# Strassen stage of a two-layer expert network: ScalarE copies the sixth product's bank ahead of the first tile's relu

## The chip, the cores and the metric

The kernel runs on one core of one Trainium2 chip. The metric is the time of one execution of the whole program in microseconds; lower is better. The engines are named as in the profile: PE is TensorE (PEld its weight loads), DVE is VectorE, ACT is ScalarE, POOL is GpSimd, SP is SyncE.

## The reference

Three networks follow one another: pooled attention, a leaky two-layer network, and four experts whose outputs are added with weights. The change lies in the last one.

```
def _moe2_ref(x, domain_probs, w1, w2):
    p = domain_probs / (domain_probs.sum(-1, keepdims=True) + 1e-09)
    out = np.zeros((N, D))                  # N 1152, D 512, 4 experts, F 1024
    for e in range(E):
        h = np.maximum(x @ w1[e], 0.0)
        out += p[:, e:e + 1] * (h @ w2[e])
    return out
```

## The kernel before

Every matrix product is made in three parts: an operand is split into a high half, which ACT writes (helper `hi`, line 91), and the rest, which DVE or POOL subtracts (helper `lo`, line 98); then high times high, high times low and low times high are added up in PSUM. The instructions stand in each engine's queue in the order in which the program calls them; no scheduler moves them.

The expert stage takes the hidden columns in 16 pairs of tiles of 128 (`NPAIR`), numbered p, four pairs to an expert. For one pair the product x @ w1 is made by Strassen's scheme in the Winograd form: seven products of half size instead of eight. `product(p, name)` issues one: 12 weight loads and 12 matmuls of 288 columns (line 688), and the instructions that empty its bank pair. They run in the order P1, P5, P2, P6, P3, P7, P4, so P7 is the sixth and P4 the seventh.

PSUM has four bank pairs here: `x0` and `x1` (by p % 2), `v` and `z`. P1, P6, P7 and P4 of one pair add up in one x pair of banks; after each, its sum so far is copied out before the next is added:

- P1: ACT copies it to the first half of `ca` (line 694). P5: ACT copies it to `c5` (tile cc, line 696). P2: DVE adds its bank to the first half of `ca` (line 698).
- P6: ACT copies the x banks to the second half of `ca` (line 700). P3: DVE adds its bank to that half (line 702). Now `ca` holds the pair's first tile, f1: ACT writes its relu to the tile gg (line 704), and DVE the low part of it (line 705).
- P7: ACT copies the x banks to `cb` (line 707), and DVE adds `c5` (line 708).
- P4 adds into the same x banks, so its first matmul waits for the copy of line 707. Its bank and `cb` make the second tile, f2: ACT relu (line 712), DVE low part (line 713), once for each half.

The order of the products is a list written by the program. P4 of a pair does not follow its P7 at once. After a pair with odd p, P1 of the next pair stands between. After a pair with even p above 0, one of nine output tiles stands between (`second_moe2`, lines 728 to 730: 12 matmuls of 512 columns, with DVE adding the result to `oacc` on line 735), and the eight others follow P4. Pair 0 is like an odd one. In the last pair, p = 15, P4 comes straight after P7, and after it the last nine output tiles, which read both tiles of pairs 14 and 15.

Weights of later pairs are prepared between: `prep_w1` after P5 and P6 (ACT `hi` and DVE `lo`, tile ws), `sums_w1` on POOL (lines 651 to 654), `prep_w2` after P2 of the next pair, or after P7 in the last pair (ACT `hi`, POOL `lo`, tile bb).

Of the kernel before, what the change touches and what calls it, by code (L numbers as in the profile page):

```python
# [33 lines left out]
def f32(ap):  # L34
    return ap.bitcast(F32)
# [3 lines left out]
def tile_kernel(ctx: ExitStack, tc: tile.TileContext, q, k, v, w_in, w_out, probs, w1, w2, out):  # L39
    nc = tc.nc  # L40
    PE, ACT, DVE, POOL, SP = nc.tensor, nc.scalar, nc.vector, nc.gpsimd, nc.sync

    def at(name, off, shape, dt=F32R):

        return nc.alloc_sbuf_tensor_at(name, [128, *shape], dt, offset=BASE + 4 * off).ap()
# [40 lines left out]
    cb, c5 = at("cb", 50560, [SQ], F32), at("cc", 52384, [SQ], F32)  # L86
# [106 lines left out]
    with ExitStack() as actx:  # L193
# [247 lines left out]
        with tc.manual_schedule():  # L441
# [65 lines left out]
            for i, (n, t) in enumerate(tiles):  # L507
# [16 lines left out]
                if t in (1, 4, 6, 8):  # L524
                    name, w = {1: ("A1", 256), 4: ("A2", 320), 6: ("B1", 320), 8: ("B2", 256)}[t]
# [26 lines left out]
    def view(t, n=NC):  # L552
        return t.rearrange("p (c w) -> p c w", c=n)
# [124 lines left out]
    def product(p, name):  # L678
        x = f"x{p % 2}"
        tag, first = {"P1": (x, 1), "P6": (x, 0), "P7": (x, 0), "P4": (x, 0), "P5": ("v", 1), "P3": ("v", 0), "P2": ("z", 1)}[name]  # L680
        ps = banks[tag]
        part, i, operand = OPERAND[name]
        w, y = w1_t[p, part], yb[operand]
        for k in range(2):
            ks = slice(k * 128, (k + 1) * 128)
            for m, (wi, yi) in enumerate(((0, 0), (0, 1), (1, 0))):
                for c in range(2):
                    PE.matmul(ps[:, c, :HW], w[wi][:, i, ks], y[:, yi, k, c * HW:(c + 1) * HW],  # L688
                              start=bool(first and k == 0 and m == 0), stop=k == 1 and m == 2, skip_group_check=True)
        s = ps[:, :, :HW]  # L690
        f1, f2 = n1 + 2 * p, n1 + 2 * p + 1
        c1, c2 = view(ca[:, :SQ], 2), view(ca[:, SQ:], 2)
        if name == "P1":
            ACT.copy(c1, s)  # L694
        elif name == "P5":
            ACT.copy(view(c5, 2), s)
        elif name == "P2":
            DVE.tensor_tensor(c1, s, c1, op=ALU.add)
        elif name == "P6":
            ACT.copy(c2, s)  # L700
        elif name == "P3":
            DVE.tensor_tensor(c2, s, c2, op=ALU.add)
            gh, gl = g_t[f1] = tuple(gg_b[2 * p % 6][:, i] for i in range(2))
            ACT.activation(gh, ca, AF.Relu)
            DVE.scalar_tensor_tensor(gl, ca, 0.0, f32(gh), op0=ALU.max, op1=ALU.subtract)
        elif name == "P7":
            ACT.copy(view(cb, 2), s)  # L707
            DVE.tensor_tensor(cb, cb, c5, op=ALU.add)
        else:
            gh, gl = g_t[f2] = tuple(gg_b[(2 * p + 1) % 6][:, i] for i in range(2))  # L710
            for src, h, l in ((s, view(gh[:, :SQ], 2), view(gl[:, :SQ], 2)), (cb, gh[:, SQ:], gl[:, SQ:])):
                ACT.activation(h, src, AF.Relu)
                DVE.scalar_tensor_tensor(l, src, 0.0, f32(h), op0=ALU.max, op1=ALU.subtract)
# [70 lines left out]
    with tc.manual_schedule():  # L784

        order, pending = [], None
        for p in range(NPAIR):
            todo = [(product, p, x) for x in ("P1", "P5", "P2", "P6", "P3", "P7")]
            order.append(todo.pop(0))
            if pending:  # L790
                order.append(pending)
            order += todo
            pending = (product, p, "P4")
            if p % 2 == 0 and p:
                tiles2 = [(second_moe2, p // 2 - 1, t) for t in range(NTT)]
                order += [tiles2[0], pending, *tiles2[1:]]
                pending = None
# [11 lines left out]
        for what, *args in order:  # L809
            what(*args)  # L810
            if what is product:
                p, name = args
# [39 lines left out]
```

## Time and profile before

| what | value |
|---|---|
| runs, us | 866.94, 868.99, 868.78; median 868.78 |
| profiled execution, us | 866.99 |
| its span, first to last instruction, us | 865.2 |
| busy over the span | PE 829.0 us (96%), PEld 777.9 (90%), DVE 587.4 (68%), ACT 435.6 (50%), POOL 403.6 (47%) |
| mean granted TensorE clock | 0.988 of full |
| Strassen and output stage | from about 470 us to the end |

Busy time is a mean over three unlike stages, and a matmul's end is modelled, so PE's 96% does not say that PE never waits. How long PE really stood still is read from the weight loads: each matmul has one, they are issued at a steady pace, and a gap in that pace is time lost.

### The profile page before, as it was taken

The page shows a single profiled execution, that of the slowest core. Times are in us where ns is not written, and L with a number is a line of the kernel's source. Part 1 is how long each engine was busy: PE and PEld are TensorE (multiplying, and loading weights), DVE is VectorE, ACT ScalarE, POOL GpSimd, SP SyncE. Part 2 cuts the span into 40 slices and gives each one's busy share as a digit, 9 for nine tenths or more (in the row PEclk, how much of TensorE's full clock was granted, in tenths as well). Part 3 has the DMA queues.
Part 4 walks back from the last instruction along what each step waited for, and adds up shares of the span by engine and source line. Part 5 has one row for each costly group of instructions (what it writes and reads, how often), then busy time and mean ns, then how long its engine had stood idle before and what let it go on. Part 6 is the DMA issues. An engine that isn't in the chain of part 4 may idle for free.

```text
span 865.2 us, 13539 instructions
## 1 busy us (share of the span) xinstructions
PE 829.0 (96%) x5071; PEld 777.9 (90%) x5071; DVE 587.4 (68%) x964; ACT 435.6 (50%) x762; POOL 403.6 (47%) x362
## 2 busy tenths in 40 slices
PE   6899999999989799999999899999999999999998
PEld 5789999999989799999999888889898898889886
DVE  5989999999998989877866662625444352625342
ACT  4889999999875565443333541505142241506030
POOL 1678988898744678556551330505032331404020
PEclk7999999999999999999999999999999999999999
DMA  6446545654501223322120210202011110201012
GB/s 192 111 123 179 136 113 151 178 125 123 153 26 50 98 98 98 98 98 74 57 91 1 72 51 1 98 1 73 26 49 49 49 50 1 98 0 49 1 37 98
DMA packets 25153, 68.65 MB, mean 79 GB/s; under 512 B 2944, under 2 KB 7040, under 8 KB 25088
## 3 DMA queue, kind: packets, MB, share of 16 engines
q1 hardware_dynamic: 25088, 67.79, 26.3%
q8 instruction: 40, 0.66, 0.3%
q14 instruction: 25, 0.20, 0.1%
HBM read 48.91 MB, written 2.36 MB: 59 GB/s over the span
## 4 chain that ended last, share of the span: by engine, by line
PE 75%; DVE 15%; ACT 4%; issue 3%; DMA 1%; POOL 1%; SPq 0%; DVEq 0%; ACTq 0%; POOLq 0%
PE ps L688 16%; PE ps L728 8%; PE ps L729 8%; PE ps L730 8%; PE ps L346 7%; PE ps L413 6%; PE ps L386 5%; DVE e L349 4%; PE ps L585 3%; PE ps L586 3%; PE ps L587 3%; PE ps L187 3%; PE ps L188 3%; PE ps L189 3%; DVE tl L98 2%
## 5 line engine op out<-in xcount | busy, mean ns | idle before, releaser
L98 POOL TENSOR_TENSOR bb<-w2r,bb 128x512 fp32r<-128x512 f32 x32 | 44.9, 1424 | 284.1 <-ACT bb L91 284.1
L688 PE MATMUL ps<-yT,ws 128*128 128x288 f32 x768 | 114.4, 300 | 10.6 <-ACT cb L707 10.6
L688 PEld LDWEIGHTS ps<-yT,ws 128*128 128x128 f32 x768 | 106.4, 191 | 15.1 <-ACT cb L707 14.9
L735 DVE SCALAR_TENSOR_TENSOR oacc<-ps,pw,oacc 128x512 f32<-128x512 f32 x63 | 47.2, 750 | 102.6 <-PE ps L730 102.6
L365 POOL TENSOR_SCALAR e<-e,st 128x1152 f32<-128x1152 f32 x70 | 86.8, 1243 | 57.4 <-DVE st L363 49.8
L98 DVE TENSOR_TENSOR tl<-ps,th 128x384 fp32r<-128x384 f32 (+1 forms) x240 | 112.0, 503 | 1.7 <-ACT th L390 1.7
L728 PE MATMUL ps<-bb,gg 128*128 128x512 f32 x288 | 112.2, 390 | 0.0
L729 PE MATMUL ps<-bb,gg 128*128 128x512 f32 x288 | 112.2, 389 | 0.0
L730 PE MATMUL ps<-bb,gg 128*128 128x512 f32 x288 | 112.1, 389 | 0.0
L346 PE MATMUL ps<-k,qst 128*128 128x384 f32 x438 | 97.2, 354 | 11.9 <-DVE e L349 6.7
L349 DVE TENSOR_SCALAR_CACHE_REDUCE e<-ps 128x1152 f32<-128x1152 f32 x72 | 97.4, 1353 | 16.3 <-PE ps L346 14.5
L390 ACT CAST th<-ps 128x384 fp32r<-128x384 f32 (+1 forms) x240 | 91.1, 458 | 23.8 <-PE ps L386 22.2
L355 ACT ACTIVATE e<-e,st 128x1152 f32<-128x1152 f32 x72 | 91.1, 1265 | 4.4 <-DVE e L349 2.7
L346 PEld LDWEIGHTS ps<-k,qst 128*128 128x128 f32 x438 | 77.4, 195 | 17.2 <-DVE e L349 11.9
L694 ACT COPY ca<-ps 128x576 f32<-128x576 f32 x16 | 10.3, 641 | 163.4 <-PE ps L688 155.0
L386 PE MATMUL ps<-ident,e 128*128 128x128 f32 x648 | 84.4, 275 | 3.8 <-POOL e L365 2.0
L688 PE MATMUL ps<-yB,ws 128*128 128x288 f32 x576 | 84.4, 296 | 0.0
L386 PEld LDWEIGHTS ps<-ident,e 128*128 128x128 f32 x648 | 75.0, 141 | 9.7 <-POOL e L365 5.0
L688 PEld LDWEIGHTS ps<-yB,ws 128*128 128x128 f32 x576 | 79.8, 189 | 0.5
L98 DVE TENSOR_TENSOR ws<-wf,ws 128x768 fp32r<-128x768 f32 (+1 forms) x32 | 41.5, 1297 | 55.5 <-ACT ws L91 55.5
L187 PE MATMUL ps<-xh,a 128*128 128x384 f32 x192 | 65.1, 339 | 4.1 <-DVE gf L564 4.1
L585 PE MATMUL ps<-g,b 128*128 128x384 f32 x192 | 64.4, 335 | 0.7 <-DVE gf L564 0.3
(126 smaller groups left out, 1728.2 us busy)
## 6 DMA issues: line engine op xcount, KB each, us to landing
wa<-in_w_in SPq DMA_DIRECT2D x16, 512.0 KB, 3.5
wb<-in_w_out SPq DMA_DIRECT2D x16, 512.0 KB, 4.3
wf<-in_w SPq DMA_DIRECT2D x32, 256.0 KB, 3.5
w2r<-in_w SPq DMA_DIRECT2D x16, 512.0 KB, 3.5
qst<-rq SPq DMA_DIRECT2D x28, 288.0 KB, 4.5
rv<-in_v SPq DMA_DIRECT2D x8, 576.0 KB, 5.3
rk<-in_k SPq DMA_DIRECT2D x7, 576.0 KB, 6.1
rq<-in_q SPq DMA_DIRECT2D x7, 576.0 KB, 4.7
```

The costliest lines, as they stand in the source:

```text
L98: eng.tensor_tensor(dst, src, f32(high), op=ALU.subtract)
L187: PE.matmul(ps[:, c, :CW], wh[:, k_], src_h[:, k_, cs], start=k_ == 0, stop=False)
L346: PE.matmul(ps[:, c, :CW], x, y, start=m == 0, stop=m == len(mms) - 1)
L349: DVE.tensor_scalar(e, ps[:, :, :CW], -0.5 / float(D) ** 0.5, None, op0=ALU.mult, op1=ALU.min, accum_out=st[:, 0:1])
L355: ACT.activation(e, e, AF.Exp, bias=st[:, 0:1], scale=-1.0, accum_out=st[:, 1:2])
L386: PE.transpose(ps[:, j], e[:, (3 * g + j) * 128:(3 * g + j + 1) * 128], ident)
L390: ACT.copy(h, ps[:, :, s0:s0 + w])
L585: PE.matmul(ps[:, c, :CW], wh, gh[:, cs], start=f == fs[0], stop=False)
L688: PE.matmul(ps[:, c, :HW], w[wi][:, i, ks], y[:, yi, k, c * HW:(c + 1) * HW], start=bool(first and k == 0 and m == 0), stop=k == 1 and m = ...
L728: PE.matmul(ps, gh[:, ts_], wh, start=f == fs[0], stop=False)
L729: PE.matmul(ps, gh[:, ts_], wl, start=False, stop=False)
L730: PE.matmul(ps, gl[:, ts_], wh, start=False, stop=f == fs[-1])
```

## The change

In `product`, the relu of the first tile and its low part (lines 704 and 705) move from the branch of P3 to the branch of P7, behind the copy of P7's bank. The same instructions are issued, as many as before.

```diff
         elif name == "P3":
             DVE.tensor_tensor(c2, s, c2, op=ALU.add)
+        elif name == "P7":
+
+            ACT.copy(view(cb, 2), s)
             gh, gl = g_t[f1] = tuple(gg_b[2 * p % 6][:, i] for i in range(2))
             ACT.activation(gh, ca, AF.Relu)
             DVE.scalar_tensor_tensor(gl, ca, 0.0, f32(gh), op0=ALU.max, op1=ALU.subtract)
-        elif name == "P7":
-            ACT.copy(view(cb, 2), s)
             DVE.tensor_tensor(cb, cb, c5, op=ALU.add)
```

The lines below move down by one: the copy is now line 705, the relu 707, the low part 708, the add of c5 709.

ACT's queue from P6 of pair 1 to P4 of pair 1, where P1 of pair 2 stands between P7 and P4 (L694 is that P1's copy; ws are weights, gg the relu's tiles):

```order
 L700 COPY ca<-ps 128x576
 L91 CAST ws_131<-wf_144 128x1024
-L704 ACTIVATE gg_138<-ca 128x1152
-L707 COPY cb<-ps 128x576
-L694 COPY ca<-ps 128x576
-L712 ACTIVATE gg_139<-ps 128x576
-L712 ACTIVATE gg_139<-cb 128x576
+L705 COPY cb<-ps 128x576
+L707 ACTIVATE gg_138<-ca 128x1152
+L694 COPY ca<-ps 128x576
+L713 ACTIVATE gg_139<-ps 128x576
+L713 ACTIVATE gg_139<-cb 128x576
```

The copy and the relu have changed places; the copy of the next pair's P1 and the two relus of the second tile stay behind both. It is the same in each of the 16 pairs.

ACT's queue at the end of the last pair, before (bb are the output weights of pair 15):

```order
552 L700 COPY ca<-ps 128x576
553 L704 ACTIVATE gg_136<-ca 128x1152
554 L707 COPY cb<-ps 128x576
555 L91 CAST bb_134<-w2r 128x512
556 L91 CAST bb_135<-w2r 128x512
557 L712 ACTIVATE gg_137<-ps 128x576
558 L712 ACTIVATE gg_137<-cb 128x576
```

and with the change:

```order
552 L700 COPY ca<-ps 128x576
553 L705 COPY cb<-ps 128x576
554 L707 ACTIVATE gg_136<-ca 128x1152
555 L91 CAST bb_134<-w2r 128x512
556 L91 CAST bb_135<-w2r 128x512
557 L713 ACTIVATE gg_137<-ps 128x576
558 L713 ACTIVATE gg_137<-cb 128x576
```

Here the two casts of the output weights stand behind the relu, which now stands behind the copy. The order on DVE, PE, POOL and SP is as before.

## Rows read from the trace of the kernel before

**Rows 1.** Page, chain that ended last: share of the span by engine.

```profile
PE 75%; DVE 15%; ACT 4%; issue 3%; DMA 1%; POOL 1%; SPq 0%; DVEq 0%; ACTq 0%; POOLq 0%
```

**Rows 2.** Waits, 465 to 866 us: engine, tile, line <- releaser: us, times, longest.

```profile
PEld ps L688 <- ACT cb L707: 14.9, 15, 2.1
...
PE ps L688 <- ACT cb L707: 10.6, 9, 1.9
```

**Rows 3.** Timeline, PE's weight loads: start us, us, instruction [idle before <- releaser].

```profile
590.16 1.66 PEld L688 LDWEIGHTS ps<-yT,ws 128*128 128x128 f32 x12
591.76 1.66 PEld L688 LDWEIGHTS ps<-yB,ws 128*128 128x128 f32 x12
594.74 3.21 PEld L688 LDWEIGHTS ps<-yT,ws 128*128 128x128 f32 x24 [1.32 <-ACT cb L707]
597.89 1.66 PEld L688 LDWEIGHTS ps<-yB,ws 128*128 128x128 f32 x12
```

**Rows 4.** Timeline of ACT in the same place.

```profile
592.99 1.16 ACT L704 ACTIVATE gg<-ca 128x1152 fp32r<-128x1152 f32 x1 [2.52 <-DVE ca L702]
594.06 0.62 ACT L707 COPY cb<-ps 128x576 f32<-128x576 f32 x1
595.75 0.64 ACT L694 COPY ca<-ps 128x576 f32<-128x576 f32 x1 [1.07 <-DVE gg L705]
596.63 0.65 ACT L712 ACTIVATE gg<-ps 128x576 fp32r<-128x576 f32 x1 [0.23 <-PE ps L688]
...
598.23 0.64 ACT L696 COPY cc<-ps 128x576 f32<-128x576 f32 x1 [0.38 <-PE ps L688]
...
599.50 1.15 ACT L91 CAST bb<-w2r 128x512 fp32r<-128x512 f32 x2
601.43 0.64 ACT L700 COPY ca<-ps 128x576 f32<-128x576 f32 x1 [0.79 <-PE ps L688]
```

**Rows 5.** Weight loads of P4 behind an output tile.

```profile
607.29 1.63 PEld L688 LDWEIGHTS ps<-yT,ws 128*128 128x128 f32 x12 [0.38 <-ACT cb L707]
```

**Rows 6.** Weight loads of the first pair's P4, with P1 of the next pair ahead.

```profile
479.97 1.66 PEld L688 LDWEIGHTS ps<-yB,ws 128*128 128x128 f32 x12
483.76 4.74 PEld L688 LDWEIGHTS ps<-yT,ws 128*128 128x128 f32 x24 [2.13 <-ACT cb L707]
```

**Rows 7.** Windows: us, PE, PEld, DVE, ACT, POOL busy (count), PE clock, DMA.

```profile
484.00:486.00 2.00, 2.00 (x10) 2.00 (x10) 1.24 (x2) 0.64 (x1) 0.00 (x0) 0.50 0.00 0
```

**Rows 8.** Timeline of ACT at the end of the last pair.

```profile
833.42 1.17 ACT L704 ACTIVATE gg<-ca 128x1152 fp32r<-128x1152 f32 x1 [1.82 <-DVE ca L702]
834.49 0.62 ACT L707 COPY cb<-ps 128x576 f32<-128x576 f32 x1
835.07 1.14 ACT L91 CAST bb<-w2r 128x512 fp32r<-128x512 f32 x2
```

**Rows 9.** Weight loads there: P7, P4, and an output tile's eleventh.

```profile
832.23 1.66 PEld L688 LDWEIGHTS ps<-yT,ws 128*128 128x128 f32 x12
835.16 1.61 PEld L688 LDWEIGHTS ps<-yT,ws 128*128 128x128 f32 x12 [1.27 <-ACT cb L707]
...
838.95 0.19 PEld L729 LDWEIGHTS ps<-bb,gg 128*128 128x128 f32 x1
```

**Rows 10.** Timeline of POOL there: low parts of the output weights.

```profile
828.99 2.53 POOL L98 TENSOR_TENSOR bb<-w2r,bb 128x512 fp32r<-128x512 f32 x2 [32.15 <-ACT bb L91]
835.77 3.13 POOL L98 TENSOR_TENSOR bb<-w2r,bb 128x512 fp32r<-128x512 f32 x2 [4.24 <-ACT bb L91]
```

**Rows 11.** Timeline of DVE there.

```profile
834.62 1.36 DVE L705 SCALAR_TENSOR_TENSOR gg<-ca,gg 128x1152 fp32r<-128x1152 f32 x1 [1.23 <-ACT gg L704]
835.89 1.85 DVE L708 TENSOR_TENSOR cb<-cb,cc 128x576 f32<-128x576 f32 x1
```

**Rows 12.** Timeline of POOL in the middle: two adds of one size.

```profile
591.23 1.60 POOL L652 TENSOR_TENSOR wf<-wf 128x256 f32<-128x256 f32 x1
592.91 0.74 POOL L653 TENSOR_TENSOR wf<-wf 128x256 f32<-128x256 f32 x1
```

## The prediction, made before the changed kernel was run

> **What bounds the kernel now.** I read the chain of waits first: three quarters of the chain that ended last is PE [rows 1], so a microsecond in which PE stands still is a microsecond of the span, unless something else is late too. Next the list of waits over the Strassen stage, to see what makes PE stand still there: nearly one thing only, the copy of the sixth product's bank (tile cb, line 707). The weight loads waited for it 15 times, 14.9 us in all [rows 2]. Matmul rows show 9 of these waits and 10.6 us; a matmul's end is modelled, so I count in weight loads.
>
> Then one such place. Behind P7 (590.16) and the next pair's P1 (591.76) P4 could load at 593.36, since a product takes 591.76 - 590.16 = 1.60 us; it loads at 594.74 [rows 3]. The copy it waits for ran from 594.06 to 594.68, although P7 had long been done: ACT was busy with the relu, and that had itself waited for DVE's add of P3, with ACT idle for 2.52 us [rows 4]. So the copy stands in ACT's queue behind an instruction whose data come later than its own. The change swaps the two.
>
> When would the copy run? ACT gets a product's result 0.34 us after the next product's weight loads begin (597.89 to 598.23, the P5 copy) [rows 3, 4]. For P7 that is 591.76 + 0.34 = 592.10; the copy takes 0.62 and ends at 592.72. P4 can load at 593.36: the wait is gone with 0.6 us to spare. The relu's data come at 592.99, after the copy, so the relu is not later.
>
> **The change part by part.** The number and length of instructions stay. What changes is four kinds of wait.
>
> (a) P4 behind P1, pairs 1, 3, ... 13: seven places. Lost now: 594.74 - 591.76 - 1.60 = 1.38 us, of which 0.05 comes back, as the two products behind it load in 597.89 - 594.74 = 3.15 instead of 3.20 us [rows 3]. 7 x 1.33 = **9.3 us**.
>
> (b) P4 behind an output tile, six places that wait. The tile covers more; weight loads wait 0.38 us [rows 5]. PE's matmul rows show no idle time there (their 9 waits are the seven, the first and the last), so the loss lies between 0 and 0.38; the load rows are the issued ones and I take 0.25. 6 x 0.25 = **1.5 us** (0 to 2.3). Put first, the copy ends 0.34 + 0.62 = 0.96 us after the tile's weight loads begin, inside a tile that lasts longer than a product.
>
> (c) Pair 0. P4 loads at 483.76 instead of 479.97 + 1.60 = 481.57: 2.19 us. And its 24 weight loads take 4.74 us, where the same 24 take 3.21 elsewhere [rows 3, 6]: the granted clock is 0.50, the 1.2 GHz level, just then [rows 7]. Ahead of the fall PE had stood still for 2.13 us; behind the 1.32 us waits it did not fall. The copy needs P7's result at 479.97 + 0.34 = 480.31 and ends at 480.93, before 481.57. With the wait gone I expect the full clock: another 4.74 - 3.21 = 1.53. Together **3.7 us** (2.2 if the clock falls all the same).
>
> (d) The last pair. P4 follows P7 at once, and no weights are prepared, so P3's sum is ready before P7's result. P7's result comes at 832.23 + 1.60 + 0.34 = 834.17 [rows 9]; now the relu starts at 833.42 and is out of the way at 834.49, the copy follows [rows 8]. With the change the copy runs from 834.17 to 834.79, so P4 starts about 0.3 us earlier. But the relu waits behind it. On ACT an instruction starts some 0.09 us before the row of the one ahead ends (592.99 + 1.16 = 594.15 against 594.06 [rows 4]), so the relu starts at 834.70 instead of 833.42, **1.28 us late**. Behind the relu are the casts of the output weights: 835.77 instead of 835.07, 0.70 late, and POOL's low parts behind these start at 836.47 instead of 835.77 [rows 8, 10]. POOL's two ended at 838.90, and the load that reads the second ran at 838.95 [rows 9, 10]: no slack. So PE's output tile will wait for POOL. POOL's two take 2.53 us where DVE is quiet, 3.13 here [rows 10], with DVE's add of c5 beside them stretched to 1.85 [rows 11]; and a POOL add beside a long DVE split took 1.60 against 0.74 [rows 12], 0.8 more. DVE's low part of f1 (1.36) would now run from about 835.9 to 837.3, over POOL's start. The end comes at 836.47 + 2.53 = 839.0 at best and 836.47 + 3.13 + 0.8 = 840.4 at worst: 0.1 to 1.5 us lost. I take 1.4, near the worst, since both engines will be busy. **-1.4 us**.
>
> What is late next? First the chain that the relu starts: low part on DVE, then ACT's copy of the next P1 (595.75, after its wait for that DVE step), which the next P6 must see before it adds into the bank. It ends at 596.39 as now; P6, now at 597.89 + 1.60 = 599.49, comes 1.33 earlier, at 598.16: 1.77 us spare. Second, the copy of P6 (601.43): its product would be done at 600.10. Ahead of it ACT works from 595.75 to 600.65 [rows 4], less the idle 0.23 and 0.38 in it, that is until 600.04: just in time. It ends at 600.74, and the next P7 begins at 594.74 + 5 x 1.60 - 0.05 - 1.33 = 601.36: 0.6 us spare. DVE, POOL and the loads follow PE's products and move with them.
>
> Sum: 9.3 + 1.5 + 3.7 - 1.4 = 13.1 us. The profiled execution took 866.99 (span 865.2 and 1.8 around it), which gives 853.9. It is the second fastest of four: the median of the runs shown is 868.78, 1.79 above, which gives 855.7. What those 1.79 us are the trace does not say; I take **854.6**, between the two.
>
> **The rivals.** *The clock stays low in pair 0* (0.13): the fall there follows a stand of PE that the change removes, but it is one event in one execution. Then 854.6 + 1.5 = 856.1.
>
> *A new wait at the next link* (0.13): the 0.6 us before P7 and ACT's queue before the P6 copy are tight. If that copy came 1.1 us later, P7 would wait 0.5 us in seven pairs: 854.6 + 3.5 = 858.1. For it: ACT is without a gap there. Against it: the rows put the copy ahead of P7.
>
> *The relu is held back, and the time gets longer* (0.03): the copy, put first, waits for P7, and everything behind it on ACT waits too. If P7 came after P3's sum in every pair, as it does in the last one, relu, low part and the next P1's copy would slip, and PE would wait at the next P6 instead of at P4. It decides from a slip of 1.77 us on. To lose what is gained and be 0.3% slower, PE would have to wait (13.1 + 2.6) / 8 = 2.0 us at each of the eight places without an output tile, a slip of 3.7 us: about 871.5. Against it: in the middle the copy is over at 592.72 and the relu's data come at 592.99, a slip of nothing; the last pair's slip is 1.28. The Trainium skill has the rule behind this rival ("PSUM — Partial Sum Buffer", section "Engine vs sequencer instructions"): the queues of ScalarE and VectorE are strict first-in first-out, so that an instruction whose data are there cannot pass one that waits. By that rule the change could cost in any pair what it costs in the last; the trace agrees that nothing passes, for the copy of line 707 sat behind the relu for some 2 us, and this is also why swapping helps.
>
> *The wait is not the copy's* (0.03): releasers are inferred; if P4 waited for something else that comes at the same time, nothing changes: 867 to 869. Against it: in each place looked at P4 loads about 0.05 us after the copy's end.
>
> **How the numbers follow.** The forecast has 0.68. Within it: (b) 0 to 2.3, (d) 0.1 to 1.5 and the two bases move the time from 852 to 857; with the clock rival and most of the new-wait rival the range is **851.5 to 858.0**. About 0.3%, 2.6 us, is what a measurement of this kernel can tell from no change. Faster by more: 0.68 + 0.13 + 0.13 = 0.94. Same: 0.03. Slower: 0.03.
>
> **What would show it.** Right: the list of waits no longer has weight loads waiting for the copy of cb, but for one of some 0.9 us in the last pair; the copy starts some 0.3 us after P1's weight loads begin, ahead of the relu; the relu still waits for DVE's add; around 484 us the clock stays at 1.00; near the end one output tile waits for POOL by up to 1.5 us. Wrong: PE waiting for the copies of P1 or P6 (lines 694 and 700), a relu whose releaser is the copy or PE in the middle pairs, or a clock that falls elsewhere.

## The result, and the profile after

The changed kernel takes 854.54 us in the median of four runs (853.84 to 857.0), the kernel before, in the same comparison, 867.92 (866.94 to 868.99): ratio 0.985, 95% interval 0.983 to 0.988. A second comparison gave 854.38 (852.88 to 854.66) against 866.72 and a ratio of 0.986 (0.984 to 0.988). So the change makes the kernel 1.2 to 1.7% faster. The prediction was 854.6, range 851.5 to 858.0.

The profiled execution took 853.91 us with a span of 852.1, against 866.99 and 865.2. All of it lies in the Strassen stage: from the first weight load of that stage to the end are 852.1 - 470.31 = 381.8 us, before 865.2 - 470.24 = 394.9 (with the span's second decimal), **13.1 us less**, where the sum of the prediction said 13.1.

The chain of waits on the page of the changed kernel, which answers to [rows 1]:

```profile
PE 78%; DVE 14%; issue 3%; ACT 2%; DMA 2%; POOL 1%; POOLq 0%; SPq 0%; DVEq 0%; ACTq 0%
```

PE holds more of the chain, ACT half of what it held. The list of waits over the Strassen stage, which answers to [rows 2] (engine, tile, line <- releaser: us in total, times, longest):

```profile
ACT cb L705 <- PE ps L688: 26.2, 16, 2.6
...
ACT gg L707 <- DVE ca L702: 3.9, 9, 1.1
...
PEld ps L730 <- POOL bb L98: 1.8, 2, 1.2
...
PEld ps L688 <- ACT cb L705: 1.0, 1, 1.0
PE ps L688 <- ACT cb L705: 0.8, 1, 0.8
PE ps L730 <- POOL bb L98: 0.8, 1, 0.8
```

Of 15 waits for the copy of cb, 14.9 us, one is left, 1.0 us, in the last pair. What is new are two waits of an output tile for POOL, 1.8 us. ACT had idled 39.6 us in all before the relu, for its data; in the kernel before the list has

```profile
ACT gg L704 <- DVE ca L702: 39.6, 16, 3.0
```

Now it idles 3.9 us there, and 26.2 us ahead of the copy, which waits for P7's result.

One place in the middle, the counterpart of [rows 3, 4]. ACT's timeline:

```profile
585.43 0.64 ACT L705 COPY cb<-ps 128x576 f32<-128x576 f32 x1 [1.67 <-PE ps L688]
586.29 1.17 ACT L707 ACTIVATE gg<-ca 128x1152 fp32r<-128x1152 f32 x1 [0.22 <-DVE ca L702]
589.07 0.64 ACT L694 COPY ca<-ps 128x576 f32<-128x576 f32 x1 [1.61 <-DVE gg L708]
```

and the weight loads there (P7, P1 of the next pair, P4 with P5):

```profile
583.45 1.66 PEld L688 LDWEIGHTS ps<-yT,ws 128*128 128x128 f32 x12
585.05 1.66 PEld L688 LDWEIGHTS ps<-yB,ws 128*128 128x128 f32 x12
586.65 3.26 PEld L688 LDWEIGHTS ps<-yT,ws 128*128 128x128 f32 x24
```

P4 loads 586.65 - 585.05 = 1.60 us after P1: no wait. The copy starts 0.38 us after P1's loads begin and ends at 586.07; then ACT idles 0.22 us more for DVE's add, and only then can the relu start. It is not later than it was: from P7's first load to the relu 586.29 - 583.45 = 2.84 us, before 592.99 - 590.16 = 2.83 [rows 3, 4]. In pairs 0 to 14 the trace gives DVE's add, not the copy, as what releases the relu. The copy fitted into a gap in which ACT had nothing to do.

Pair 0, the counterpart of [rows 6, 7], the weight loads and the clock (windows: us, busy PE, PEld, DVE, ACT, POOL, then the granted clock):

```profile
480.05 1.66 PEld L688 LDWEIGHTS ps<-yB,ws 128*128 128x128 f32 x12
481.65 3.25 PEld L688 LDWEIGHTS ps<-yT,ws 128*128 128x128 f32 x24
```

```profile
484.00:486.00 2.00, 2.00 (x17) 2.00 (x16) 1.35 (x3) 1.26 (x3) 0.00 (x0) 1.00 0.04 8
```

No wait, and the clock stays at 1.00 (2.4 GHz), where it was 0.50.

The last pair, the counterpart of [rows 8 to 11]; weight loads, ACT, POOL and DVE:

```profile
817.92 1.66 PEld L688 LDWEIGHTS ps<-yT,ws 128*128 128x128 f32 x12
820.59 1.61 PEld L688 LDWEIGHTS ps<-yT,ws 128*128 128x128 f32 x12 [1.01 <-ACT cb L705]
...
824.19 0.19 PEld L730 LDWEIGHTS ps<-bb,gg 128*128 128x128 f32 x1 [0.56 <-POOL bb L98]
...
825.94 0.19 PEld L730 LDWEIGHTS ps<-bb,gg 128*128 128x128 f32 x1 [1.22 <-POOL bb L98]
```

```profile
819.90 0.64 ACT L705 COPY cb<-ps 128x576 f32<-128x576 f32 x1 [2.61 <-PE ps L688]
820.43 1.17 ACT L707 ACTIVATE gg<-ca 128x1152 fp32r<-128x1152 f32 x1
821.50 1.13 ACT L91 CAST bb<-w2r 128x512 fp32r<-128x512 f32 x2
```

```profile
822.19 3.70 POOL L98 TENSOR_TENSOR bb<-w2r,bb 128x512 fp32r<-128x512 f32 x2 [4.97 <-ACT bb L91]
```

```profile
821.63 1.36 DVE L708 SCALAR_TENSOR_TENSOR gg<-ca,gg 128x1152 fp32r<-128x1152 f32 x1 [2.56 <-ACT gg L707]
822.91 1.84 DVE L709 TENSOR_TENSOR cb<-cb,cc 128x576 f32<-128x576 f32 x1
```

Counted from P7's first load, P4 comes at 2.67 us (before 2.93), the relu at 2.51 (1.19), the casts of the output weights at 3.58 (2.84), and POOL is done with both at 7.97 (6.67). The last load that waits for POOL comes at 8.02 where it came at 6.72 [rows 9]: 1.3 us lost, and to the end of the span 1.2. (The two waits add up to 1.8, but P4 came 0.26 earlier, and the loads behind a wait follow each other faster.)

### The profile page after: what moved, and what is told of

Same layout as the page of the kernel before. It is cut to its first block, busy times and chain, and to the rows that moved or that the text cites. A ratio compares the mean times of both kernels' runs of the same rounds, so it can differ in the third digit from the quotient of the medians.

```text
span 852.1 us, 13562 instructions
## 1 busy us (share of the span) xinstructions
PE 824.6 (97%) x5071; PEld 776.6 (91%) x5071; DVE 590.1 (69%) x964; ACT 435.6 (51%) x762; POOL 412.4 (48%) x362
## 4 chain that ended last, share of the span: by engine, by line
PE 78%; DVE 14%; issue 3%; ACT 2%; DMA 2%; POOL 1%; POOLq 0%; SPq 0%; DVEq 0%; ACTq 0%
PE ps L688 20%; PE ps L730 8%; PE ps L729 7%; PE ps L731 7%; PE ps L346 7%; PE ps L413 5%; PE ps L386 5%; DVE e L349 4%; PE ps L585 3%; PE ps L586 3%; PE ps L587 3%; PE ps L187 3%; PE ps L189 3%; DVE tl L98 3%; PE ps L188 3%
## 5 line engine op out<-in xcount | busy, mean ns | idle before, releaser
L688 PE MATMUL ps<-yT,ws 128*128 128x288 f32 x768 | 111.5, 296 | 0.8 <-ACT cb L705 0.8
L694 ACT COPY ca<-ps 128x576 f32<-128x576 f32 x16 | 10.3, 641 | 167.6 <-PE ps L688 154.8
L730 PEld LDWEIGHTS ps<-bb,gg 128*128 128x128 f32 x288 | 54.1, 188 | 12.4 <-POOL bb L98 1.8
```

What stands on the lines that cost most here:

```text
L730: PE.matmul(ps, gh[:, ts_], wl, start=False, stop=False)
```

## The experiments

Since stages ahead of the change differ between executions by a few microseconds, each profile is read from the first weight load of the Strassen stage to the end of the span. In that measure the kernel before has 394.9 us, the changed one 381.8; its second profile gave 851.1 - 469.26 = 381.8 again. Of the kernels e1, e2, e3, e5 and e6 there is one execution each, so they are read by this measure alone.

> The changed kernel again, beside the two runs that it is compared with: 853 to 857 us.

Measured as said above: 854.38 us.

**One group of places at a time.** The relu and its low part are put into a helper that stands after P3's add in the old order and after P7's copy in the new, by pair:

```diff
+    NEW = (0,)              # e1;  range(1, 14, 2) e2;  range(2, 15, 2) e3;  range(15) e4
+    def relu1(p, f1):
+        gh, gl = g_t[f1] = tuple(gg_b[2 * p % 6][:, i] for i in range(2))
+        ACT.activation(gh, ca, AF.Relu)
+        DVE.scalar_tensor_tensor(gl, ca, 0.0, f32(gh), op0=ALU.max, op1=ALU.subtract)
...
             DVE.tensor_tensor(c2, s, c2, op=ALU.add)
-            gh, gl = g_t[f1] = tuple(gg_b[2 * p % 6][:, i] for i in range(2))
-            ACT.activation(gh, ca, AF.Relu)
-            DVE.scalar_tensor_tensor(gl, ca, 0.0, f32(gh), op0=ALU.max, op1=ALU.subtract)
+            if p not in NEW:
+                relu1(p, f1)
...
             ACT.copy(view(cb, 2), s)
+            if p in NEW:
+                relu1(p, f1)
```

> Only pair 0 has the new order, all others the old one. Theory (the wait for the copy is lost time, place by place): the wait of 2.1 us behind P1 of pair 1 is gone and the clock does not fall there, so the span is 3.7 us under that of the kernel before, 865.2 to 861.5; the 24 weight loads of P4 and P5 take 3.2 us. Rival (the clock falls there whatever PE did before): 2.2 us, 863.0, and the 24 loads take 4.7 us. Second rival (the wait moves on to the next pair): under 1 us.

> Only the pairs 1, 3, ... 13 have the new order, those where P1 of the next pair stands between P7 and P4. Theory: 7 times 1.33 us, 9.3 us off the span of the kernel before: 855.9. Rival (the places with an output tile between pay for it, since the tile comes earlier there): 7 us or less off, with longer waits in the even pairs than the 0.38 us of before.

> Only the pairs 2, 4, ... 14 have the new order, those with an output tile between P7 and P4. Theory: six waits of 0.38 us in the weight loads go, of which 0.25 us each counts: 1.5 us off the span of before, 863.7. Rivals: the waits are hidden by the matmuls still running, 0 us, 865.2; or they count in full, 2.3 us, 862.9.

> The changed kernel with the old order in the last pair alone. Theory (the change loses 1.2 us there, because the casts of the output weights and with them POOL's low parts come 0.7 us later and collide with DVE's low part): from P7 of the last pair to the first output result 7.6 us as in the kernel before, instead of 8.8; span 850.9 against 852.1. Rival (the 1.2 us come from the load of the output weights, which would land late in either order): no difference.

| new order in | first load to end, us | against before |
|---|---|---|
| pair 0 (e1) | 863.6 - 471.78 = 391.8 | -3.1 |
| pairs 1, 3, ... 13 (e2) | 855.7 - 470.91 = 384.8 | -10.1 |
| pairs 2, 4, ... 14 (e3) | 863.8 - 470.16 = 393.6 | -1.3 |
| all but the last (e4) | 850.0 - 469.37 = 380.6 | -14.3 |
| all (the change) | 381.8 | -13.1 |

Pair 0 alone gives 3.1 and not 3.7, but the 24 loads are at full pace (3.25 us), so the rival on the clock falls. The missing 0.6 is in the next pair. The loads of its P4 in e1 (the first 14):

```profile
496.22 1.89 PEld L695 LDWEIGHTS ps<-yT,ws 128*128 128x128 f32 x14 [1.85 <-ACT cb L714]
```

That wait was 1.32 before: the part of the gain that moved on (the second rival, in part). Adding it, pair 0 was worth 3.1 + 0.5 = 3.6. The odd pairs give more than 9.3, and here too the difference is seen in the neighbours: the waits behind an output tile, 0.38 us before [rows 5], are now

```profile
556.52 1.62 PEld L695 LDWEIGHTS ps<-yT,ws 128*128 128x128 f32 x12 [0.22 <-ACT cb L714]
```

in six of the seven (the first is 0.25; the seventh, behind pair 14, had none before). So the rival that the even places would pay is wrong in its sign. The even pairs alone give 1.3 where 1.5 was expected: both rivals, 0 and 2.3, fall. The sum of the parts, 3.1 + 10.1 + 1.3 = 14.5, is what all but the last give together, 14.3. And the old order in the last pair alone is worth 381.8 - 380.6 = 1.2 us. From P7 to the first output result it takes 7.59 us, as expected, against 8.80 in the changed kernel, so the rival that blames the load of the output weights falls. Its time is 851.76 us (851.39 to 853.77), ratio to before 0.984 (0.982 to 0.986). Whether it is faster than the changed kernel the intervals do not tell; the stage's own time does, by 1.2 us.

**The clock in pair 0.** In the kernel before, the 12 matmuls of P1 of pair 1 are issued twice:

```diff
-        for k in range(2):
+        for k in (0, 1, 0, 1) if (p, name) == (1, "P1") else (0, 1):
```

> The kernel before, but the 12 matmuls of P1 of pair 1 are issued twice, so that PE works for 1.6 of the 2.1 us in which it stood before P4 of pair 0. Theory (the clock fell because PE had stood): P4 still waits for the copy and loads at the same time, but the clock stays at full speed and the 24 loads behind take 3.2 instead of 4.7 us: with more work the span is 1.5 us shorter, 863.7. Rival (the fall has another cause): 24 loads in 4.7 us and a span of 865.2; or, if the doubled product delays others, longer.

The weight loads (the doubled P1, then P4 with P5):

```profile
478.57 3.25 PEld L695 LDWEIGHTS ps<-yB,ws 128*128 128x128 f32 x24
482.35 3.23 PEld L695 LDWEIGHTS ps<-yT,ws 128*128 128x128 f32 x24 [0.53 <-ACT cb L714]
```

P4 loads 3.78 us after P1 began, as before (483.76 - 479.97 = 3.79), but the 24 loads take 3.23 instead of 4.74 us. From the first load to the end: 862.3 - 468.84 = 393.5 us, 1.5 less than before, with more work. So the stand of PE had cost 1.5 us more than its own length, through the clock, and the theory holds. One execution could be chance, but the other profiles side with it: at this place the granted clock fell in all three in which PE stood for 2.13 us (the kernel before, e2, e3) and stayed at 1.00 in all eight in which it did not.

**What comes next.** The relu is issued twice in pairs 0 to 14 of the changed kernel:

```diff
         ACT.activation(gh, ca, AF.Relu)
+        if p < NPAIR - 1:
+            ACT.activation(gh, ca, AF.Relu)
```

> The changed kernel with the relu of the first tile issued twice in pairs 0 to 14, 1.07 us more on ACT each. Theory (what comes next after the removed wait is ACT's queue, which has no gap from the copy of P1 to the copy of P6 and only 0.3 to 0.4 us to spare before P7): PE waits about 0.7 us before P7 of the pairs 1, 2, 4, 6, ... 14, the eight that follow a pair without an output tile; span some 5.8 us longer, 857.9. Rival (the next link is the copy of P1 before P6, with 1.77 us to spare): no wait in these pairs, span 852 to 853.

From the first load to the end 853.8 - 469.56 = 384.3 us, 2.4 more than the changed kernel: neither 5.8 nor nothing. The waits of the weight loads (L709 is here the copy of P6):

```profile
484.09 1.66 PEld L697 LDWEIGHTS ps<-yB,ws 128*128 128x128 f32 x12
485.87 1.60 PEld L697 LDWEIGHTS ps<-yT,ws 128*128 128x128 f32 x12
487.52 1.62 PEld L697 LDWEIGHTS ps<-yB,ws 128*128 128x128 f32 x12
489.83 1.60 PEld L697 LDWEIGHTS ps<-yT,ws 128*128 128x128 f32 x12 [0.69 <-ACT ca L709]
...
501.94 1.61 PEld L697 LDWEIGHTS ps<-yT,ws 128*128 128x128 f32 x12 [0.69 <-ACT ca L709]
...
594.20 1.66 PEld L697 LDWEIGHTS ps<-yB,ws 128*128 128x128 f32 x12
595.96 1.60 PEld L697 LDWEIGHTS ps<-yT,ws 128*128 128x128 f32 x12
```

At the first two places P7 waits the expected 0.7 us for the copy of P6. There the rival's link gives way too, by less: P6 loads at 485.87, 0.18 us late, right behind the copy of P1:

```profile
485.18 0.64 ACT L703 COPY ca<-ps 128x576 f32<-128x576 f32 x1 [1.48 <-DVE gg L685]
```

Together each of the two costs about 0.9 us. At the six others the load of P7 is late by only 595.96 - 594.20 - 1.60 = 0.16 us, of which 0.05 comes back behind it. The spare time was misjudged by taking the first places for all: there the relu starts later, since in the changed kernel ACT idles for DVE's add 1.06 and 0.78 us after the copy, and 0.23 or less in the later pairs. 2 x 0.9 + 6 x 0.1 = 2.4, the whole cost. The copy of P6 is the link with the least to spare, 0.3 to 0.4 us at two places and about 1 us at six; the copy of P1 comes next.

**A version that beats both.** In the changed kernel, the output weights of pair 14 are prepared ahead of P1 of pair 15, those of pair 15 after its P6:

```diff
         for what, *args in order:
+            if what is product and tuple(args) == (NPAIR - 1, "P1"):
+                prep_w2(NPAIR - 2)
+                load_w2(NPAIR - 1)
             what(*args)
...
                     ahead_w1(p + 1, 1)
-                elif name == "P2" and p or name == "P7" and p == NPAIR - 1:
+                    if p == NPAIR - 1:
+                        prep_w2(p)
+                elif name == "P2" and 0 < p < NPAIR - 1:
```

> The changed kernel with the output weights of pair 14 prepared ahead of P1 of pair 15 instead of after its P2, and those of pair 15 after its P6 instead of after its P7, so that POOL has them ready long before the last output tiles. Theory: no wait for POOL is left at the end, P4 still waits some 1.0 us for the copy; from P7 to the first output result 7.3 us, span 850.6. Rival (DVE's part is as late: low part, add of c5 and low part of the second tile follow one another): a wait for DVE of about 1 us takes its place, span 851.6.

POOL's low parts, and DVE's add of c5 (L717 here), in this kernel:

```profile
817.43 2.52 POOL L98 TENSOR_TENSOR bb<-w2r,bb 128x512 fp32r<-128x512 f32 x2 [6.42 <-ACT bb L91]
```

```profile
822.46 0.75 DVE L717 TENSOR_TENSOR cb<-cb,cc 128x576 f32<-128x576 f32 x1
```

No wait for POOL is left, and none for DVE takes its place. From P7 to the first output result it takes 7.31 us. First load to end: 850.2 - 469.87 = 380.3 us, 1.5 less than the change, as expected; 851.97 us (851.18 to 852.94), ratio to before 0.984 (0.982 to 0.986). The one wait left, P4 for the copy, 1.01 us, is covered by cutting the first two of the last nine output tiles:

```diff
-        order += [pending, *[(second_moe2, NPAIR // 2 - 1, t) for t in range(NTT)]]
+        G = NPAIR // 2 - 1
+        order += [(second_moe2, G, 0, 0), pending, (second_moe2, G, 1, 0), (second_moe2, G, 0, 1), (second_moe2, G, 1, 1)]
+        order += [(second_moe2, G, t) for t in range(2, NTT)]
```

(`second_moe2` takes a half, issues the six matmuls of that pair, and adds to `oacc` after the second.)

> The kernel with the early casts, and the first two of the last nine output tiles cut in halves: the six matmuls of tile 0 that read pair 14 stand between P7 and P4 of pair 15, those of tile 1 right behind P4. Theory (the one wait left is P4's for the copy, 1.0 us, and the half tile of 1.36 us covers it): no wait for the copy is left, and from the first weight load of the Strassen stage to the end 379.3 us instead of 380.3. Rival (the second tile's relu and low part become late instead, since they start from P4's result): a wait for ScalarE or VectorE of 0.5 to 1 us takes its place, 380.

P4's loads, behind the half tile, carry no wait:

```profile
820.92 1.74 PEld L695 LDWEIGHTS ps<-yT,ws 128*128 128x128 f32 x12
```

First load to end 849.7 - 470.44 = 379.3 us, as expected. The list of waits of this kernel has no wait of PE or of its weight loads in the whole stage. 851.6 us (849.93 to 852.63) against 867.98 in the same comparison, ratio 0.981 (0.980 to 0.983): the shortest stage of the kernels run. (By the medians alone, 851.6, 851.76 and 851.97 us, it cannot be told from the two kernels ahead of it.) Against the changed kernel it gains 2.5 us in the stage; its interval, 0.980 to 0.983, lies under that of the changed kernel in its second comparison, 0.984 to 0.988, and touches that of the first, 0.983 to 0.988; the two were never run in one comparison.

## Why the prediction was right

- **What bounds the kernel**: PE's stands in this stage were the copy's. When the copy no longer waits behind the relu, 14 of 15 waits are gone, and the time falls by what they had cost.
- **(a) seven places behind P1, 9.3 us** and **(b) six behind an output tile, 1.5 us**: measured 9.3 and 1.3. In the load rows of the changed kernel P4 follows P1 in 1.60 us at each of the seven places, before in 2.98, and 0.05 is given back: 1.33, as said. At the six places it follows the tile in 2.65 instead of 2.99, and 0.12 is given back behind it: 0.22 where 0.25 was taken, between the bounds. e3 measures (b) alone, 1.3. e2 gives more than (a), since a place that is shortened also moves its neighbour's wait, 0.38 to 0.22.
- **(c) pair 0, 3.7 us**: 3.1 alone, and 0.5 that had moved on to pair 1. The clock's part, 1.5, is shown by e5 by itself; the rival that the clock falls all the same is refuted by e1 and by the changed kernel. That the relu is not later holds at the places like the one worked out; in pairs 1 and 2 it starts 0.52 and 0.44 us later after P7's first load, behind a later add of DVE.
- **(d) the last pair, -1.4 us**: measured -1.2. Each step came as worked out: P4 earlier by 0.26 (0.3 said), relu later by 1.32 (1.28), casts and POOL's start later by 0.74 and 0.73 (0.70). POOL's two took 3.70 us, between the 2.53 and the 3.93 of the bounds. The 2.53 was read as POOL's time "where DVE is quiet"; one DVE add of a PSUM bank ran beside it.
- **What is late next**: the copy of P6 does follow a gapless run of ACT at the first two places; in a later one ACT idles 0.24 us ahead of it. In the changed kernel it ends 0.37 us before P7's loads at one of the first two places (499.84 + 0.64 against 500.85), where the prediction worked out 0.6 for one place and took it for all (0.63 in a later one, 593.38 + 0.64 against 594.65); e6 shows that this gives way first, and the copy of P1 next. The rival of a new wait there did not happen, but two of its places were nearer than said.
- **The relu held back**: in the middle its slip is nothing (2.84 against 2.83 us after P7's first load), in the last pair 1.32. The rule of strict order on ScalarE's queue costs only where the relu's data come before P7's result, and that is the last pair.
- **The sum and the base**: that the stage is 13.1 us shorter, as summed, owes something to luck, for (b) was 0.2 us too large and (d) 0.2 us too low. That 854.6 lies so near the measured 854.54 is luck altogether: the base was taken halfway between two, and what parts them was not known. It is still open. In the nine executions of the kernel before in the second comparison the mean granted clock goes along with the time, from 0.993 at 864.48 and 864.66 us to 0.987 and 0.988 at 866.96 to 868.18. One place where the clock differs lies in the leaky network, near 296 us. In the changed kernel's first profile PE stood there for 2.94 us, and the clock fell behind it:

```profile
296.49 0.28 PEld L187 LDWEIGHTS ps<-xh,a 128*128 128x128 f32 x1 [2.94 <-DVE gf L564]
```

```profile
296.00:300.00 4.00, 3.51 (x12) 3.51 (x13) 4.00 (x7) 3.53 (x5) 1.79 (x2) 0.57 0.41 131
```

In its second, an execution 1.0 us shorter with the same time in the Strassen stage, PE stood as long and the clock did not fall:

```profile
296.05 0.19 PEld L187 LDWEIGHTS ps<-xh,a 128*128 128x128 f32 x1 [2.94 <-DVE gf L564]
```

```profile
296.00:300.00 4.00, 3.95 (x22) 3.95 (x23) 4.00 (x6) 3.80 (x5) 1.77 (x2) 1.00 0.37 131
```

From this load to the first of the Strassen stage are 173.8 us in the first profile and 173.2 in the second, so this fall makes up 0.6 of the 1.0 us. The profile of the kernel before has it too (0.57), so it is no part of the 13.1.

## What to carry to other kernels

On an engine that works in order, look at pairs of neighbours in its queue: if the one ahead regularly waits for data while the other's are there, and the busiest engine waits for the other, swap them. The price is read from the waits of the busiest engine for the second (14.9 us in the weight loads here, and 13.1 were gained), not from the idle time before the first (39.6 us). Then look for the places where the data come in the other order, as in the last pair here: there the same swap delays a chain, and the place is best left as it was, or its chain started earlier. And price a stand of TensorE by the pace of the loads behind it too, not by its length alone: one of 2.1 us cost 3.7. Read that pace from the trace, since in some executions other stands here, longer ones too, left the clock at full speed.

## What was not expected of the hardware

DVE's add of two SBUF tensors (576 columns) takes 0.75 us alone and 1.84 or 1.85 beside POOL's low parts, in three kernels, and POOL's two take 2.52 us alone, 3.12 or 3.13 in the old order and 3.70 in the new one. Single rows of the changed kernel read as if each waited for the other's whole instruction (read from the rows, not tested by a run):

```profile
822.19 1.95 POOL L98 TENSOR_TENSOR bb<-w2r,bb 128x512 fp32r<-128x512 f32 x1 [4.97 <-ACT bb L91]
824.10 1.79 POOL L98 TENSOR_TENSOR bb<-w2r,bb 128x512 fp32r<-128x512 f32 x1
```

DVE's add starts at 822.91, inside POOL's first, and ends 0.6 us after it (822.91 + 1.84 against 822.19 + 1.95); POOL's second ends 1.1 us after DVE's add. A DVE instruction with one of its operands in PSUM is not stretched, though it runs wholly inside POOL's second:

```profile
824.68 0.74 DVE L714 SCALAR_TENSOR_TENSOR gg<-ps,gg 128x576 fp32r<-128x576 f32 x1
```

The Trainium skill states when the two collide ("SBUF — State Buffer", section "Who interferes with whom": a VectorE instruction with two SBUF inputs contends with a GpSimd instruction that reads SBUF, for a shared port pair that it calls an exclusive lock); the trace agrees, with 0.75 against 1.84 us, and 0.74 for the one that reads PSUM. Of the 1.3 us by which POOL is done later in the last pair, 0.73 is its later start and 0.57 the longer collision, 3.70 against 3.13 us. With the early casts POOL's low parts are over before DVE's add of c5, and PE waits for neither.

The granted clock fell behind a stand of PE of 2.13 us (three profiles with the old order in pair 0), but not behind one of 1.85 us (e1) or of 0.53 (e5). The length alone does not decide: behind the stand of 2.9 us near 296 us it fell in six of the eleven profiles and stayed at 1.00 in five, and behind one of 2.3 to 2.4 us near 42 us it fell in two and stayed at 1.00 in nine. What decides, these runs do not tell, nor how often the fall of pair 0 would be missing over more executions of the kernel before.
